# Moving transfers within one issue queue: q tiles two iterations later, the w2 pieces, g2T and pqT at other f chunks, and the first reload of hh in two transfers

## Chip, cores, metric

One core of one Trainium2 chip. The metric is the device time of one execution in microseconds (us); the span of the profile is some 1.7 us shorter. A difference under 2% counts as "same"; the 95% intervals say which differences are clear of noise. One kernel's executions differ by several us from chip to chip and from run to run (the kernel before: 854.9 to 856.5 on one chip). So times are compared only with the kernel before in the same rounds on the same chip, and parts of a microsecond are read from the traces, stretch by stretch.

## The reference

A transformer layer, forward and backward, in bf16, S = 2048 rows, D = 640, 32 heads, F = 1728:

```
h   = x + linear_attention(layernorm(x)) @ wo     # phi(q), phi(k), phi(k)^T v per head
out = h + (silu(n @ w1) * (n @ w3)) @ w2           # n = layernorm(h)
return out, gradients of x, wqkv, wo, w1, w3, w2   # for a given grad_out
```

## The kernel before

The schedule is written by hand. Nearly all DMAs are issued by SP in program order (`dma`, and `dmaT` for a transposing DMA). In the first stage x is normalised, transposed and multiplied by wqkv. From row tile 8 on, the transposes of x (`xn` to `pqT`) are DMAs:

```python
    def p1_norm(t):
        xns[t] = p1.tile([P, D], BF16, name="xn", bufs=4)
        ln1.norm(xns[t][:], x_sb[:, t, :], t)
        if t >= XT_DMA:                                   # 8
            dmaT(out=pqT[:, :, t * P:(t + 1) * P], in_=xns.pop(t)[:])
    # ...
    for t in range(ST):
        # ... k tile, v tile, a kv group every fourth t
        if XT_DMA <= t + 3 < ST:
            p1_norm(t + 3)
        if t + 4 < ST:
            ln1.run(x_sb, t + 4, t + 5)
        if 4 <= t < 12:
            q_tile(t - 4)                                 # ends with a store of pq
        if t in (9, 13):
            load_pqT((t - 9) // 4)                        # transposing reload of 4 stored q tiles
        # ...
        if i == TPC - 1:
            sl = slice(g * TPC, (g + 1) * TPC)
            dma(out=pk_v[:, sl, :], in_=pkc[g][:])
            dma(out=va_v[:, sl, :], in_=va[g % 2][:])
        elif t >= 2 and trickle:
            trickle.pop(0)()                              # one weight load
```

The second stage is the MLP over four chunks c of 512 rows, in 14 f chunks each. Beside it runs the attention output of the next chunk: per row tile `nd` (matmul), `o_t` (DVE), its transpose `oT` (DMA), the out-projection `at` (matmul), `hn` and its transpose.

```python
        for fc in range(FT):
            mlp(c, fc, lambda: run_side(0, fc))
            # ... stores of hh, gate and up are dealt out between these
            run_side(1, fc)
            drain(1)
            if c == 0 and fc in (1, 4, 7):
                a, b = {1: (0, 4), 4: (4, 8), 7: (8, 13)}[fc]
                dma(out=w2[:, a:b, :], in_=B_w2[a * P:b * P, :].rearrange("(c p) n -> p c n", p=P))
                # ...
            if c < 2 and fc == 11:
                load_pqT(c + 2)
            if fc == (9 if c == 0 else 3) and c + 1 < SC:
                load_g2T(c + 1)
            # ...
    def load_hh(b):
        f0, fw = blk[b]
        hb[b] = U2.tile([P, ST, 512], BF16, name="hb", tag="ABCA"[b])
        dmaT(out=hb[b][:, :, 0:fw], in_=hh_d[f0:f0 + fw, :])
    load_hh(0)
```

After that come the gradient of w2 (`gw`, reads hb), the gradient of hn (`ghn`, reads ggb), the attention's gradients (`gwo` and others) and the remaining weight gradients.

Of the kernel before, what the change touches and what calls it, by code (L numbers as in the profile page):

```python
# [9 lines left out]
P = 128  # L10
# [15 lines left out]
W, SC, TPC = 512, 4, 4  # L26
# [37 lines left out]
def kernel(  # L64
# [20 lines left out]
    dma, dmaT = SY.dma_start, SY.dma_start_transpose  # L85
# [18 lines left out]
    hh_d = dram.tile([F, S], BF16, name="hh_d")  # L104
# [68 lines left out]
    def make_mask(m):  # L173
        a, b = M_H[m]
        v = mask[:, m, 0:M_W[m]]
        G.memset(v, 1.0)
        v = v.rearrange("p (h e) -> p h e", e=DA)

        G.affine_select(out=v, in_=v, pattern=[[-DH, b - a], [0, DA]], compare_op=ALU.is_ge, fill=0.0,
                        base=m * P - a * DH, channel_multiplier=1)  # L180
        G.affine_select(out=v, in_=v, pattern=[[DH, b - a], [0, DA]], compare_op=ALU.is_gt, fill=0.0,
                        base=a * DH + DH - m * P, channel_multiplier=-1)
# [9 lines left out]
    def load_g2T(c):  # L192
        g2T[c] = U2.tile([P, DT, W], BF16, name="g2T", tag="g2T", bufs=2)
        dmaT(out=g2T[c][:], in_=goD[c * W:(c + 1) * W, :])

    def load_pqT(c):
        dmaT(out=pqT[:, :, c * W:(c + 1) * W], in_=pq_d[c * W:(c + 1) * W, :])
# [16 lines left out]
# [3 lines that stand above are left out]
        if t >= XT_DMA:  # L217
            dmaT(out=pqT[:, :, t * P:(t + 1) * P], in_=xns.pop(t)[:])

    def p1_tr(t):  # L220
        xn = xns.pop(t)
        tr = ps.tile([P, DT, P], BF16, name="tr", bufs=2)
        for c in range(DT):
            T.transpose(tr[:, c, :], xn[:, c * P:(c + 1) * P], ident[:])

        A.copy(out=pqT[:, :, t * P:(t + 1) * P], in_=tr[:])
# [6 lines left out]
    def p1_mm(t, n0):  # L233
        acc = ps.tile([P, 2, 512], F32, name="big", bufs=3)
        for j in range(2):
            p1_half(acc[:, j, 0:HD], t, n0 + j * HD)
        return acc
# [4 lines left out]
    def phi(acc, dst, relu=False):  # L242
        mq = p1.tile([P, D], BF16, name="mq", bufs=3)
        A.activation(two(mq[:]), acc[:, :, 0:HD], AF.Exp)
        if relu:
            rq = p1.tile([P, D], BF16, name="rq", bufs=3)
            A.activation(two(rq[:]), acc[:, :, 0:HD], AF.Relu)
        V.tensor_scalar(out=mq[:], in0=mq[:], scalar1=1.0, scalar2=1e-6, op0=ALU.min, op1=ALU.add)
        if relu:
            V.tensor_tensor(out=dst, in0=mq[:], in1=rq[:], op=ALU.add)  # L250
            return
        V.scalar_tensor_tensor(out=two(dst), in0=acc[:, :, 0:HD], scalar=0.0, in1=two(mq[:]), op0=ALU.max,
                               op1=ALU.add)

    def q_store(t, pq):
        dma(out=pq_v[:, t, :], in_=pq)

    def q_tile(t):
        pq = p1.tile([P, D], BF16, name="pq", bufs=3)
        phi(p1_mm(t, 0), pq[:], True)  # L260
        q_store(t, pq[:])

    def kv_group(g, last):
        kv = ps.tile([P, 2, 512], F32, name="big", bufs=3)
        for i in range(TPC):
            for m, (a, b) in enumerate(M_H):
                bank, off = KV_SLOT[m]
                T.matmul(kv[:, bank, off:off + M_W[m]], lhsT=pkc[g][:, i, m * P:(m + 1) * P],
                         rhs=va[g % 2][:, i, a * DA:b * DA], start=(i == 0 and off == 0), stop=(i == TPC - 1),
                         skip_group_check=True)  # L270
        for bank, w in ((0, sum(M_W[0:3])), (1, sum(M_W[3:5]))):
            if g == 0:
                V.tensor_copy(out=kvacc[:, bank, 0:w], in_=kv[:, bank, 0:w])
            else:
                V.tensor_tensor(out=kvacc[:, bank, 0:w], in0=kvacc[:, bank, 0:w], in1=kv[:, bank, 0:w],
                                op=ALU.add)
        if last:
            for m, (a, b) in enumerate(M_H):
                bank, off = KV_SLOT[m]
                V.tensor_tensor(out=kvbd[:, m, a * DA:b * DA], in0=kvacc[:, bank, off:off + M_W[m]],  # L280
                                in1=mask[:, m, 0:M_W[m]], op=ALU.mult)
# [22 lines left out]
    for t in range(ST):  # L304
        g, i = divmod(t, TPC)
        if i == 0:
            pkc[g] = p1.tile([P, TPC, D], BF16, name="pkc", bufs=2)
        k = p1_mm(t, D)
        if t + 2 < XT_DMA:
            p1_norm(t + 2)  # L310
        phi(k, pkc[g][:, i, :])
        if t + 1 < XT_DMA:
            p1_tr(t + 1)
        if i == 0 and g > 0:
            kv_group(g - 1, False)
        v = p1_mm(t, 2 * D)
        A.copy(out=va[g % 2][:, i, 0:C].rearrange("p (j h e) -> p j h e", j=2, e=DA)[:, :, :, 0:DH],
               in_=v[:, :, 0:HD].rearrange("p j (h e) -> p j h e", e=DH))
        if XT_DMA <= t + 3 < ST:
            p1_norm(t + 3)  # L320
        if t + 4 < ST:
            ln1.run(x_sb, t + 4, t + 5)
        if 4 <= t < 12:
            q_tile(t - 4)
        if t in (9, 13):
            load_pqT((t - 9) // 4)
        if 2 <= t < 2 + DT:
            make_mask(t - 2)
            G.memset(kvbd[:, t - 2, :], 0.0)
# [5 lines that stand above are left out]
            trickle.pop(0)()  # L335
# [150 lines left out]
    def drain(n):  # L486
        for _ in range(min(n, len(later))):
            later.pop(0)()
# [74 lines left out]
    for c in range(SC):  # L563
        hhT[c] = pa.tile([P, FT, W], BF16, name="hhT", bufs=2)
        o2 = o2_steps(c - 1) if c > 0 else None

        def run_side(pos, fc):
            if c + 1 < SC:
                for f, i in sorted(sides[c][pos].get(fc, ()), key=lambda x: x[1]):
                    f((c + 1) * TPC + i)  # L570
# [4 lines that stand above are left out]
            if o2 and not (c == SC - 1 and fc == 5):  # L575
                next(o2, None)
            run_side(1, fc)
            drain(1)
            if c == 0 and fc in (1, 4, 7):
                a, b = {1: (0, 4), 4: (4, 8), 7: (8, 13)}[fc]  # L580
                dma(out=w2[:, a:b, :], in_=B_w2[a * P:b * P, :].rearrange("(c p) n -> p c n", p=P))
                if fc == 7:
                    dma(out=w2[0:FL, FT - 1, :], in_=B_w2[(FT - 1) * P:F, :])
            if c < 2 and fc == 11:
                load_pqT(c + 2)
            if fc == (9 if c == 0 else 3) and c + 1 < SC:
                load_g2T(c + 1)
            if c == SC - 1 and fc == 0:
                g2 = U1.tile([P, ST, D], BF16, name="g2", tag="Q")
                tail = U2.tile([P, DT, P], BF16, name="w13tail", tag="g2T", bufs=2)  # L590
            if c == SC - 1 and fc in (1, 2, 5, 6):
                i = (1, 2, 5, 6).index(fc)
                dma(out=g2[:, i * TPC:(i + 1) * TPC, :], in_=goS[:, i * TPC:(i + 1) * TPC, :])
            if c == SC - 1 and fc == 8:
                dma(out=tail[:, :, 0:FL], in_=B_w1[:, F - FL:F].rearrange("(c p) f -> p c f", p=P))
                dma(out=tail[:, :, FL:P], in_=B_w3[:, 0:P - FL].rearrange("(c p) f -> p c f", p=P))
            if c == SC - 1 and fc == 9:
                woT = U1.tile([P, DT, D], BF16, name="woT", tag="W6")
                dmaT(out=woT[:], in_=A_wo[:, :])
# [5 lines left out]
    hb, blk = {}, [(0, 512), (512, 512), (1024, 512), (1536, 192)]  # L605

    def load_hh(b):
        f0, fw = blk[b]
        hb[b] = U2.tile([P, ST, 512], BF16, name="hb", tag="ABCA"[b])
        dmaT(out=hb[b][:, :, 0:fw], in_=hh_d[f0:f0 + fw, :])  # L610

    load_hh(0)
    for _ in o2_steps(SC - 1, A.dma_start, "nd"):
        drain(1)
# [56 lines left out]
    for fc in range(FT - 1):  # L671
        b, i = divmod(fc, 4)
# [252 lines left out]
    a, b, c = ST - 1, ST - 2, ST - 3  # L925
# [103 lines left out]
    for t in range(ST):  # L1029
        c, i = divmod(t, TPC)  # L1030
# [124 lines left out]
```

## Time and profile before

| | before |
|---|---|
| time, median | 855.38 us (854.9 to 856.47, 4 runs) |
| span of the profile | 852.4 us |
| TensorE busy | 837.7 us |
| waits of TensorE that the change can reach | xn 1.4, hb 1.1, g2T 0.6, nd 0.3 us |

TensorE does almost nothing but work. What is left are gaps of about 1 us where it waits for one transfer, and the prediction below quotes them. A line of waits reads: engine, what it wanted to do, the line, what it waited for, then the sum, the number and the longest. PE is TensorE, DVE VectorE, ACT ScalarE, and SPq the queue of SyncE, here called SP.

### The profile page before, as it was taken

The page shows a single profiled execution, that of the slowest core. Times are in us where ns is not written, and L with a number is a line of the kernel's source. Part 1 is how long each engine was busy: PE and PEld are TensorE (multiplying, and loading weights), DVE is VectorE, ACT ScalarE, POOL GpSimd, SP SyncE. Part 2 cuts the span into 40 slices and gives each one's busy share as a digit, 9 for nine tenths or more (in the row PEclk, how much of TensorE's full clock was granted, in tenths as well). Part 3 has the DMA queues.
Part 4 walks back from the last instruction along what each step waited for, and adds up shares of the span by engine and source line. Part 5 has one row for each costly group of instructions (what it writes and reads, how often), then busy time and mean ns, then how long its engine had stood idle before and what let it go on. Part 6 is the DMA issues. An engine that isn't in the chain of part 4 may idle for free.

```text
span 852.4 us, 14861 instructions
## 1 busy us (share of the span) xinstructions
PE 837.7 (98%) x5908; PEld 543.3 (64%) x5908; DVE 415.5 (49%) x951; ACT 322.2 (38%) x608; POOL 31.7 (4%) x57
## 2 busy tenths in 40 slices
PE   6999999999999999999999999999999999999998
PEld 4776654555555555677777777777877777655554
DVE  7876698777778566200146666554413343300000
ACT  4656866555555665011111211122522333311111
POOL 2510000000000000000000000000000000000000
PEclk9999999999999999999999999999999999999999
DMA  9999379465574555999679999979666887677671
GB/s 284 270 303 268 104 209 240 140 176 142 128 192 128 156 176 157 242 232 255 181 167 187 204 204 208 172 143 264 145 132 128 191 199 162 159 168 155 154 175 37
DMA packets 344949, 156.35 MB, mean 183 GB/s; under 512 B 247600, under 2 KB 343600, under 8 KB 344880
## 3 DMA queue, kind: packets, MB, share of 16 engines
q1 hardware_dynamic: 316064, 142.45, 69.5%
q10 hardware_dynamic: 28816, 12.97, 7.9%
q8 instruction: 46, 0.75, 0.4%
q14 instruction: 23, 0.19, 0.1%
HBM read 45.20 MB, written 50.02 MB: 112 GB/s over the span
## 4 chain that ended last, share of the span: by engine, by line
PE 81%; DMA 6%; DVE 2%; ACT 1%; ACTq 0%; issue 0%; SPq 0%; DVEq 0%
PE job L986 21%; PE mm L429 18%; PE ghn L734 9%; PE gxn L1076 8%; PE gw L678 7%; PE o L520 6%; PE gwo L841 3%; PE at L386 2%; DMA ggb<-gg_d 2%; PE h L791 2%; DMA hb<-hh_d 2%; DMA ghT<-g_h 1%; PE mm L230 1%; PE dkv L1035 1%; PE dkv L822 1%; DMA pqT<-pq_d 1%
## 5 line engine op out<-in xcount | busy, mean ns | idle before, releaser
L986 PE MATMUL job<-gb,hnN 128*128 128x432 bf16 x640 | 117.0, 346 | 0.0
L734 PEld LDWEIGHTS <-ggb 128*128 128x128 bf16 x864 | 83.0, 98 | 31.9 <-DMA ggb<-gg_d 1.1
L986 PEld LDWEIGHTS <-hnN 128*128 128x128 bf16 x640 | 62.6, 98 | 54.1
L429 PE MATMUL mm<-pqT,w 128*128 128x512 bf16 x405 | 96.1, 379 | 0.0
L429 PEld LDWEIGHTS <-w 128*128 128x128 bf16 x540 | 52.4, 98 | 60.7 <-issue 0.2
L990 ACT CAST obs<-job 128x432 bf16<-128x432 f32 (+1 forms) x70 | 33.3, 475 | 123.8 <-PE job L986 123.8
L429 PE MATMUL mm<-g2T,w2T 128*128 128x512 bf16 x280 | 69.6, 379 | 0.6 <-DMA g2T<-in_grad_out_dram 0.6
L520 PE MATMUL o<-w,hhT 128*128 128x320 bf16 x448 | 67.5, 299 | 0.0
L1076 PE MATMUL gxn<-wqT,gT 128*128 128x320 bf16 x480 | 67.3, 299 | 0.0
L734 PE MATMUL ghn<-w13a,ggb 128*128 128x320 bf16 x448 | 65.6, 299 | 0.0
L734 PE MATMUL ghn<-w13b,ggb 128*128 128x320 bf16 x416 | 63.5, 299 | 0.6 <-DMA ggb<-gg_d 0.4
L230 PE MATMUL big<-wqkv,pqT 128*128 128x320 bf16 x400 | 57.8, 303 | 2.3 <-DMA pqT<-xn 1.4
L230 PEld LDWEIGHTS <-pqT 128*128 128x128 bf16 x480 | 46.5, 99 | 20.9 <-DMA pqT<-xn 2.1
L520 PEld LDWEIGHTS <-hhT 128*128 128x128 bf16 x448 | 43.8, 98 | 23.6
L678 PE MATMUL gw<-g,hb 128*128 128x320 bf16 x416 | 57.7, 299 | 1.1 <-DMA hb<-hh_d 1.1
L1076 PEld LDWEIGHTS <-gT 128*128 128x128 bf16 x480 | 47.0, 98 | 18.2
L986 PEld LDWEIGHTS <-g 128*128 128x128 bf16 x480 | 46.6, 98 | 17.5
L446 ACT CAST ghh<-mm 128x512 bf16<-128x512 f32 x56 | 32.8, 586 | 64.3 <-PE mm L429 63.9
L757 ACT ACTIVATE y<-wb,s,ln_rs 128x640 bf16<-128x640 f32 x32 | 29.4, 920 | 66.5 <-DVE wb L753 66.5
L678 PEld LDWEIGHTS <-hb 128*128 128x128 bf16 x416 | 40.2, 98 | 16.6 <-DMA hb<-hh_d 1.4
L745 ACT ACTIVATE gs<-ghn 128x640 bf16<-128x640 f32 x16 | 11.3, 704 | 88.6 <-PE ghn L734 74.0
L460 ACT ACTIVATE sig<-mm 128x512 bf16<-128x512 f32 x56 | 33.5, 598 | 28.8 <-PE mm L429 27.7
(139 smaller groups left out, 1062.3 us busy)
## 6 DMA issues: line engine op xcount, KB each, us to landing
hh_d<-hhT SPq DMA_DIRECT2D x24, 256.0 KB, 2.5
gg_d<-gate SPq DMA_DIRECT2D x24, 256.0 KB, 2.5
gg_d<-up SPq DMA_DIRECT2D x24, 256.0 KB, 2.5
ggb<-gg_d SPq DMA_DIRECT2D x6, 896.0 KB, 8.0
ggb<-gg_d SPq DMA_DIRECT2D x6, 832.0 KB, 8.2
out_dram<-obs ACTq DMA_DIRECT2D x40, 108.0 KB, 1.9
ggb<-gg_d SPq DMA_DIRECT2D x2, 1728.0 KB, 13.0
va_d<-va SPq DMA_DIRECT2D x4, 768.0 KB, 6.6
```

What stands on the lines that cost most here:

```text
L230: T.matmul(acc, lhsT=pqT[:, c, t * P:(t + 1) * P], rhs=wqkv[:, c, n0:n0 + HD], start=(c == 0), stop=(c == DT - 1))
L429: T.matmul(acc[:], lhsT=w[:, c, fc * P:(fc + 1) * P], rhs=rhs[:, c, :], start=(c == 0), stop=(c == DT - 1))
L446: A.copy(out=ghh[n // 2][:, n % 2, :], in_=acc[:])
L460: A.activation(sig[:, i, :], gp[:], AF.Sigmoid)
L520: T.matmul(o2["ps"][:, 0:HD], lhsT=hhT[c][:, fc, i * P:(i + 1) * P], rhs=w2[:, fc, j * HD:(j + 1) * HD], start=(fc == 0), stop=(fc == FT - 1))
L678: T.matmul(acc[:, j, 0:HD], lhsT=hb[b][:, t, i * P:(i + 1) * P], rhs=g2[:, t, j * HD:(j + 1) * HD], start=(t == 0), stop=(t == ST - 1))
L734: T.matmul(acc[:, j, 0:HD], lhsT=ggb[t // 2][:, k, lo:lo + P], rhs=rhs[:, j * HD:(j + 1) * HD], start=(k == 0), stop=(k == NG - 1))
L757: A.activation(out=y[:], in_=wb[:], func=AF.Identity, bias=s[:, 3:4], scale=st.rs[:, t:t + 1])
L841: T.matmul(acc[m][:, j, 0:HD], lhsT=o_sb[:, t, m * P:(m + 1) * P], rhs=g_h[:, t, j * HD:(j + 1) * HD], start=(t == 0), stop=(t == ST - 1))
L986: T.matmul(acc[:, 0:n], lhsT=lhs[:, t, m * P:(m + 1) * P], rhs=rhs(t), start=(t == 0), stop=(t == ST - 1))
L990: A.copy(out=ob, in_=acc[:, 0:n])
L1076: T.matmul(acc[:, j, 0:HD], lhsT=gT[t][:, k, :], rhs=wqT[:, k, j * HD:(j + 1) * HD], start=(k == 0), stop=(k == 14))
```

## The change

Its intent is to give four transfers more lead. Nothing is computed differently.

```diff
-        if 4 <= t < 12:
-            q_tile(t - 4)
-        if t in (9, 13):
-            load_pqT((t - 9) // 4)
+        if 6 <= t < 14:
+            q_tile(t - 6)
+        if t in (11, 15):
+            load_pqT((t - 11) // 4)
@@
-                a, b = {1: (0, 4), 4: (4, 8), 7: (8, 13)}[fc]
+                a, b = {1: (0, 5), 4: (5, 9), 7: (9, 13)}[fc]
@@
-            if c < 2 and fc == 11:
+            if c < 2 and fc == 10 - 2 * c:
                 load_pqT(c + 2)
-            if fc == (9 if c == 0 else 3) and c + 1 < SC:
+            if fc == (5 if c == 0 else 3) and c + 1 < SC:
                 load_g2T(c + 1)
@@ load_hh
-        dmaT(out=hb[b][:, :, 0:fw], in_=hh_d[f0:f0 + fw, :])
+        for a, n in ((0, 2 * P), (2 * P, 2 * P)) if b == 0 else ((0, fw),):
+            dmaT(out=hb[b][:, :, a:a + n], in_=hh_d[f0 + a:f0 + a + n, :])
```

## The prediction

> **What bounds the kernel now.** I read the page's header first, then the waits of TensorE, then the same engine's timeline around each wait, and last the timeline of SP, the queue that issues nearly all DMAs in program order.
>
> ```profile
> span 852.4 us, 14861 instructions
> PE 837.7 (98%) x5908; PEld 543.3 (64%) x5908; DVE 415.5 (49%) x951; ACT 322.2 (38%) x608; POOL 31.7 (4%) x57
> PE 81%; DMA 6%; DVE 2%; ACT 1%; ACTq 0%; issue 0%; SPq 0%; DVEq 0%
> ```
>
> TensorE is busy for 837.7 of 852.4 us at a granted clock of 1.00. The change adds and removes no matmul, so all that it can win is idle time of TensorE: 852.4 - 837.7 = 14.7 us, 1.7% of the span. Even the whole of it would not be 2%. The waits say how much of it the change can reach:
>
> ```profile
> PE tr L224 <- DVE xn L145: 5.6, 1, 5.6
> PE big L230 <- DMA pqT<-xn: 1.4, 2, 1.1
> PE gw L678 <- DMA hb<-hh_d: 1.1, 1, 1.1
> PE big L230 <- ACT pqT L226: 0.8, 1, 0.8
> PE mm L429 <- DMA g2T<-in_grad_out_dram: 0.6, 1, 0.6
> PE at L386 <- DVE o_t L362: 0.5, 1, 0.5
> PE ghn L734 <- DMA ggb<-gg_d: 0.4, 1, 0.4
> PE nd L349 <- DMA pqT<-pq_d: 0.3, 1, 0.3
> ```
>
> The 5.6 and the 0.8 us are the start of the kernel (first x and its normalisation), and 121.00 - 116.84 = 4.2 us lie after the last matmul (the stretch from 732 to 853 us); the change touches neither. Four of these waits are in its reach: xn (1.4), hb (1.1), g2T (0.6), nd (0.3), 3.4 us in all, 0.4% of the time. So the question is only which of these go, and what new wait a moved transfer makes.
>
> [...] the transpose of hb is 8.52 us on SP but lands 13.0 us after its start. [...] SP issues in program order, and one long transpose there (w2T, 15.17 us) holds back all issues behind it.
>
> **Part 1, q tiles two iterations later.** A q tile is ten matmuls at a pitch of 1.36/10 us, so 1.36 us of TensorE. They leave iterations 4 and 5 and appear in 12 and 13. From iteration 4 to 13 TensorE runs up to 2 x 1.36 = 2.7 us ahead of before, and from iteration 14 on it stands where it stood, less the waits saved. The timeline before:
>
> ```profile
> 59.45 1.52 PE L230 MATMUL big<-wqkv,pqT 128*128 128x320 bf16 x10
> 61.33 5.61 PE L230 MATMUL big<-wqkv,pqT 128*128 128x320 bf16 x40 [0.36 <-DMA pqT<-xn]
> 68.02 2.89 PE L230 MATMUL big<-wqkv,pqT 128*128 128x320 bf16 x20 [1.07 <-DMA pqT<-xn]
> ```
>
> Those waits are for the DMA transposes of x tiles 13 and 15. On SP tile 13's was issued at 55.51 and landed 5.8 us later, at 61.3; tile 15's at 61.60, landing 6.4 us later, at 68.0. Tile 13's was held back by the reload of pqT chunk 0 (issued at 51.16, 3.63 us on SP). This reload now comes two iterations later, so tile 13 is issued near 49.5, lands near 55, and TensorE asks for it at 59.5 (counting 1.36 us a half-tile group and 1.33 a kv group from 23.64): that wait goes. Tile 8 becomes tighter: TensorE asks for it at 36.4 instead of 39.1; before, it was issued at 32.61 behind the g2T transpose, which itself stood behind the first q store. Without that store it is issued near 30.3 and lands near 35, so no wait, with 1.5 us to spare.
>
> But the reload of chunk 0 now stands ahead of tile 15. It follows the store of q tile 5, whose matmuls end at 54.1; from the end of such matmuls to the reload's issue it took 2.6 us before (48.6 to 51.16), so the reload is issued near 56.6 and done near 60.3. Then come the stores of pk and va (about 0.6 us each), and tile 15 is issued near 61.5, as before, landing near 68.0. TensorE would ask at 66.3, now 0.65 us sooner. So I expect one wait of about 1.7 us for tile 15 in place of 0.36 + 1.07 and the two small start-up losses beside them (0.15 each): **about 0.0 us** for the stage, between -1.7 (the wait vanishes) and +0.8.
>
> **Part 2, transfers among the f chunks of the first c.** g2T for chunk 1 moves from f chunk 9 to 5. Before, it was issued at 137.26, landed 5.5 us later, and TensorE waited:
>
> ```profile
> 129.55 1.52 PE L386 MATMUL at<-wo,oT 128*128 128x320 bf16 x10 [0.46 <-DVE o_t L362]
> 142.78 1.25 PE L429 MATMUL mm<-g2T,w2T 128*128 128x512 bf16 x5 [0.64 <-DMA g2T<-in_grad_out_dram]
> 150.84 0.53 PE L349 MATMUL nd<-kvbd,pqT 128*128 128x147 bf16 x6 [0.33 <-DMA pqT<-pq_d]
> ```
>
> Issued some 15 us sooner it is there in time: -0.64 us. The reload of pqT chunk 2 goes from f chunk 11 to 10, some 5 us sooner, against a wait of 0.33: -0.33 us. For c = 1 the reload (now f chunk 8) had no wait to lose: 0. The w2 pieces (5, 4, 4 instead of 4, 4, 5) have no wait of their own: 0.
>
> The new place of g2T costs something. Its issue follows the store of hh at 121.21 on SP, just ahead of this:
>
> ```profile
> 121.21 0.37 SPq L479 DMA_DIRECT2D hh_d<-hhT  x1
> 122.17 0.37 SPq L411 DMA_DIRECT2D hn_d<-hn  x1
> 123.64 0.34 SPq L364 DMA_DIRECT2D o_d<-o_t  x1
> 124.27 0.39 SPq L479 DMA_DIRECT2D gg_d<-gate  x1
> 124.75 1.24 SPq L419 DMA_TRANSPOSE pqT<-hn  x1
> 126.05 1.27 SPq L370 DMA_TRANSPOSE oT<-o_t  x1
> ```
>
> g2T takes SP from 121.7 to 125.2. The gaps between these lines take up part of it; packed back to back (0.45 + 0.4 + 0.45 + 1.3 us) the oT transpose starts near 127.9 to 128.2 instead of 126.05. It landed 2.6 us after issue, so near 130.7 instead of 128.65. The out-projection of row tile 6 started at 129.55 (held by the DVE read of a PSUM bank), so it now starts about 1.2 us later: **+1.2 us**. Part 2 in sum: -0.64 - 0.33 + 1.2 = +0.2.
>
> **Part 3, first reload of hh in two transfers.** Its issue at 341.94 needs the last reader of w1; 13.0 us later the whole block lands, and the gradient of w2 starts at 355.04 after 1.1 us of idle. The first two f chunks need only the first half. Half the columns take about 8.52/2 = 4.3 us on SP and land another 13.0 - 8.5 = 4.5 us later, so near 350.7, while TensorE is done with its earlier work at 353.9. The second half lands near 355, and is first read two f chunks of 4.5 us later. The wait goes: **-1.1 us**. hb 1 was queued from 352.19 and is first needed at 373.1, so there is room behind.
>
> **Sum.** 0.0 + 0.2 - 1.1 = -0.9 us, mostly kept, as the later stages show only one other wait of TensorE for a DMA (0.4 us for ggb), and that transfer waits for buffers which TensorE frees, so it moves along. 855.24 - 0.9 = 854.3 us.
>
> **Rivals.** (a) All four waits vanish and nothing takes their place: -3.4, so 851.8 us. For it: each moved transfer gets more lead. Against it: SP is one queue, and in the first stage the DMA share is above 1 (1.14 from 50 to 60 us, 1.17 from 60 to 70), so what is moved back must delay something. (b) The new places hurt: the oT delay is 2 us and passes on to row tile 7 (whose oT landed 6.2 us after 130.87, at 137.07, against a use at 137.38), and tile 15 lands 1 us later. Then +0.8 + 0.9 (above the 1.2) + 0.3 offset the gain, and the time is about 854.3 + 2.0 = 856.3. For it: the margins of 0.3 and 0.9 us there. (c) The split is hidden or fails to help because the first gw matmul waits for both halves: +1.1 on the estimate, 855.4. Against it: chunks of pqT written by separate DMAs are awaited separately in this trace.
>
> **Range and chances.** From (a) to (b), with the three timed runs spread over 854.9 to 856.47, I give 852.2 to 856.4. 2% is 17.1 us, five times all waits within reach, and above all idle of TensorE; a loss of that size would need a DMA wait of a kind the trace nowhere shows. Faster 0.005, same 0.99, slower 0.005.
>
> **What would show it.** In the waits of TensorE after: hb gone, g2T and nd gone, "at" grown to 1.5 us or more and ended by oT's DMA, xn down to one wait of 1.2 to 2 us near 66 us. The oT transpose issued about 7 us after the hh store instead of 4.8. If "at" stays at 0.5, part 2 is wrong and the time is nearer 853.1; if no xn wait is left, part 1 is wrong and it is nearer 852.6. A gw wait still there would mean that the split does not free the first half.

## The result, and the profile after

855.23 us (853.45 to 856.71, 4 runs) against 855.38 us: ratio 0.9996, 95% interval 0.9973 to 1.0018. Ratios here are the mean time of one kernel's runs over that of the other's of the same rounds, so not quite the ratio of the medians. A second set of six runs (below) gave 0.9977 (0.9959 to 0.9994).

The waits of TensorE in the changed kernel:

```profile
PE tr L224 <- DVE xn L145: 5.7, 1, 5.7
PE at L386 <- DMA oT<-o_t: 2.5, 1, 2.5
PE big L230 <- ACT pqT L226: 0.8, 1, 0.8
PE h L823 <- DVE gnd L794: 0.7, 1, 0.7
PE big L230 <- DMA pqT<-xn: 0.6, 1, 0.6
```

hb, g2T and nd are gone, and xn is down from 1.4 to 0.6. The wait at the out-projection of row tile 6 grew from 0.5 to 2.5 us, and what ends it is no longer DVE but the DMA of oT. TensorE's timeline shows the three places (columns: start, length, what, and in brackets the idle time before it):

```profile
67.40 2.89 PE L230 MATMUL big<-wqkv,pqT 128*128 128x320 bf16 x20 [0.59 <-DMA pqT<-xn]
...
130.99 1.53 PE L386 MATMUL at<-wo,oT 128*128 128x320 bf16 x10 [2.51 <-DMA oT<-o_t]
...
353.94 4.51 PE L679 MATMUL gw<-g,hb 128*128 128x320 bf16 x32
```

And SP's timeline in the changed kernel shows why:

```profile
120.60 0.37 SPq L479 DMA_DIRECT2D hh_d<-hhT  x1
121.03 3.31 SPq L194 DMA_TRANSPOSE g2T<-in_grad_out_dram  x1
124.43 0.53 SPq L411 DMA_DIRECT2D hn_d<-hn  x1
...
127.32 1.27 SPq L370 DMA_TRANSPOSE oT<-o_t  x1
```

g2T keeps SP for 3.31 us, everything behind it is packed tight, and oT is issued 6.7 us after the hh store instead of 4.8 us. That is 1.9 of the 2.9 us by which oT lands later, counted from the hh store (10.35 instead of 7.48 us); the other 1.0 us is a longer time from issue to landing (3.6 instead of 2.6 us).

To see where time goes in all runs alike, I took from each timeline of TensorE the start of four groups of matmuls: the first late q tile, the first output matmul of chunk 0 (`o`), the first `gw`, `ghn` and `gwo`. Between them lie these stretches (us). From gw to ghn it is 60.3 us, and from gwo to the end 290.7 to 290.8 us, in every run; both are left out. "dip" says whether the granted clock fell in the 10 us from 130 us.

| run | q at / reload at | g2T at f chunk | split | start to late q | late q to o | dip | o to gw | ghn to gwo |
|---|---|---|---|---|---|---|---|---|
| before | 4 / 9 | 9 | no | 72.07 | 80.21 | no | 202.76 | 146.39 |
| changed | 6 / 11 | 5 | yes | 71.46 | 80.96 | no | 201.52 | 146.67 |
| e1_g2t_back | 6 / 11 | 9 | yes | 71.27 | 81.61 | no | 201.52 | 146.29 |
| e4_g2t_alone | 4 / 9 | 5 | no | 73.16 | 84.22 | 0.83 | 202.31 | 146.63 |
| e2_q_alone | 6 / 11 | 9 | no | 72.94 | 80.70 | no | 202.51 | 146.44 |
| e3_split_alone | 4 / 9 | 9 | yes | 73.10 | 79.89 | no | 201.52 | 148.11 |
| e8_g2t_fc8 | 6 / 11 | 8 | yes | 71.45 | 80.74 | no | 201.52 | 150.08 |
| e5_g2t_fc4 | 6 / 11 | 4 | yes | 72.13 | 82.17 | no | 201.52 | 146.25 |
| e6_reload_t12 | 6 / 12 | 5 | yes | 71.32 | 83.40 | 0.83 | 201.52 | 147.80 |
| e9_double | 6 / 11 | 5, doubled | yes | 73.09 | 85.53 | 0.83 | 201.52 | 146.59 |
| a1_after_again | 6 / 11 | 5 | yes | 71.20 | 83.00 | 0.83 | 201.52 | 147.32 |
| a2_after_nosplit | 6 / 11 | 5 | no | 71.89 | 83.32 | 0.83 | 202.71 | 146.48 |
| b1_order_split | 6 / 12 | 8 | yes | 70.63 | 80.11 | no | 201.52 | 146.62 |
| b2_order_nosplit | 6 / 12 | 8 | no | 70.95 | 81.27 | no | 203.02 | 146.32 |

### The profile page after: what moved, and what is told of

Read it like the earlier page. It is cut to its first block, busy times and chain, and to the rows that moved or that the text cites. A ratio compares the mean times of both kernels' runs of the same rounds, so it can differ in the third digit from the quotient of the medians.

```text
span 851.7 us, 14834 instructions
## 1 busy us (share of the span) xinstructions
PE 835.9 (98%) x5880; PEld 543.4 (64%) x5908; DVE 415.2 (49%) x951; ACT 322.1 (38%) x608; POOL 31.7 (4%) x57
## 4 chain that ended last, share of the span: by engine, by line
PE 86%; DMA 2%; DVE 1%; issue 0%; ACTq 0%; ACT 0%; SPq 0%
PE job L987 21%; PE mm L429 20%; PE ghn L735 11%; PE gxn L1077 8%; PE o L520 7%; PE gw L679 7%; PE at L386 3%; PE gwo L842 3%; PE h L792 2%; DMA ghT<-g_h 1%; PE mm L230 1%; PE dkv L1036 1%; DMA kT<-pk_d 1%; PE dkv L823 1%; PE nd L349 1%; PE h L823 1%
```

## The experiments

My theory: each part of the change wins its wait, and what it gives back comes from the order of issues on SP alone. The rivals: the transferred bytes themselves slow the neighbours wherever they stand; another part (the w2 pieces) makes the new wait; the split's gain is given back in later stages.

**e1_g2t_back** (ratio 1.0014, 0.9963 to 1.0065; one of its four runs took 862.5 us)

```diff
-            if fc == (5 if c == 0 else 3) and c + 1 < SC:   # changed kernel
+            if fc == (9 if c == 0 else 3) and c + 1 < SC:
```

> The changed kernel with g2T for chunk 1 put back to f chunk 9, everything else kept. Theory A (the g2T transpose on SP holds back the oT transpose of row tile 6): the wait of TensorE at the out-projection of tile 6 falls from 2.5 us to about 0.5 us, oT is issued about 4.8 us after the hh store (6.7 us in the changed kernel), and the g2T wait of about 0.6 us at chunk 1 comes back. Net some -1.4 us by the trace, about 850.3 us of span at full clock. Theory B (the w2 pieces of 5, 4, 4 or the later reload in the first stage made that wait): it stays near 2.5 us and the time rises by 0.6 us.

The wait at the out-projection is back at 0.46 us and the one for g2T at 0.63 us, so the w2 pieces and the later reload don't make the 2.5 us. But the net gain that I expected did not come, for a wait that I had not foreseen. TensorE's timeline of this run:

```profile
128.87 1.52 PE L386 MATMUL at<-wo,oT 128*128 128x320 bf16 x10 [0.46 <-DVE o_t L362]
...
142.09 1.25 PE L429 MATMUL mm<-g2T,w2T 128*128 128x512 bf16 x5 [0.63 <-DMA g2T<-in_grad_out_dram]
...
149.24 1.24 PE L429 MATMUL mm<-g2T,w2T 128*128 128x512 bf16 x5 [1.58 <-ACT up L468]
```

With g2T at f chunk 9 and the reload of pqT at 10, two transposes follow each other on SP (3.45 us from 136.59 and 3.81 us from 140.71). The store of up behind them comes at 144.62, ACT waits 2.5 us for its buffer, and TensorE 1.58 us for ACT. In this trace the parts of the change belong together: the earlier reload needs g2T out of the way.

**e4_g2t_alone** (1.0055, 1.0031 to 1.0078: slower than before, clear of noise)

```diff
-            if fc == (9 if c == 0 else 3) and c + 1 < SC:   # kernel before
+            if fc == (5 if c == 0 else 3) and c + 1 < SC:
```

> The kernel before with only g2T for chunk 1 moved from f chunk 9 to 5. Theory A: the g2T wait (0.6 us) goes and the wait at the out-projection of row tile 6 grows from 0.5 to about 2.4 us: net about +1.3 us, span near 853.7 us at full clock; the nd wait of 0.3 us goes too if freeing SP around 137 us lets the reload of pqT start sooner, and stays if not. Theory B: the out-projection wait stays at 0.5 us and the time falls by 0.6 us.

The wait grew to 2.88 us, a little more than forecast, but the kernel lost 4.3 us between the medians, not 1.3; the stretch from late q to o alone is 4.0 us longer (84.22 against 80.21). The g2T wait is gone; the nd wait became 1.03 us. And there is something that no wait shows: in the stretches of 10 us, the granted clock is 0.83 from 130 us on, and nowhere else in the span. The matmuls after the long wait ran slower (1.88 us for ten that take 1.52, 2.34 us for five that take 1.24).

**e2_q_alone** (1.0016, 0.9994 to 1.0038)

```diff
-        if 4 <= t < 12:                 # kernel before, other parts unchanged
-            q_tile(t - 4)
-        if t in (9, 13):
-            load_pqT((t - 9) // 4)
+        if 6 <= t < 14:
+            q_tile(t - 6)
+        if t in (11, 15):
+            load_pqT((t - 11) // 4)
```

> The kernel before with only the q tiles and their reloads two iterations later. Theory A (TensorE bound, the reload of pqT chunk 0 ahead of the tiles is what cost): two xn waits of 1.4 us in sum become one of about 0.6 us at tile 15, as in the changed kernel, and the first matmul of the late q tiles starts 0.6 us sooner than before; net -0.6 us. Theory B (the gain came by another part, or by chance from run to run): the xn waits keep a sum of 1.4 us or more.

One xn wait is left, as forecast, but it is 1.93 us, so by this run alone theory B would stand. Eight runs have the q tiles at 6 and the reload at 11; their xn waits are 0.6, 0.4, 1.9, 0.4, 0, 0.9, 0 and 0.2 us. The three with the old order have 1.4, 2.1 and 2.1 us. The late q tiles start at 71.93 us in the mean of the eight and at 72.78 us in the mean of the three: a gain of about 0.85 us, with a scatter of the same size. A single trace was too few here.

**e3_split_alone** (1.0012, 0.9990 to 1.0033)

```diff
-        dmaT(out=hb[b][:, :, 0:fw], in_=hh_d[f0:f0 + fw, :])   # kernel before
+        for a, n in ((0, 2 * P), (2 * P, 2 * P)) if b == 0 else ((0, fw),):
+            dmaT(out=hb[b][:, :, a:a + n], in_=hh_d[f0 + a:f0 + a + n, :])
```

> The kernel before with only the first reload of hh in two transfers. Theory A: the gw wait of 1.1 us goes, the first gw matmul follows the last output matmul at once (near 354.0 instead of 355.0), and 1.1 us of it is still there at the first matmul of the next stage and most at the end: span near 851.3 us. Theory B (later transfers take it back): SP's 10.7 us for the two transfers against 8.5 us for one delay w13 and ggb, the first matmul of the next stage waits, and the span is 852.4 us as before.

The gw wait is gone, and the stretch from o to gw is 201.52 us: the same to the hundredth in all nine runs with the split, and 202.31 to 203.02 in the five without. But here the ghn stage took 148.11 instead of 146.39 us, with waits of 1.3 us for ghT and 0.7 for gnd, and the gain was gone at the end. Whether that follows from the split is asked again below.

**e8_g2t_fc8** (0.9961, 0.9931 to 0.9991)

```diff
-            if fc == (5 if c == 0 else 3) and c + 1 < SC:   # changed kernel
+            if fc == (8 if c == 0 else 3) and c + 1 < SC:
```

> The changed kernel with g2T for chunk 1 at the end of f chunk 8, behind the oT transposes of row tiles 6 and 7 in SP's order, instead of 5. Theory A (only the order of SP's issues makes the wait at the out-projection of tile 6): that wait falls from 2.5 to about 0.5 us, no wait for g2T (it lands near 137 us and is read near 142), none for the reload of pqT chunk 2; from there on some 2 us sooner than the changed kernel, span near 849.8 us with the granted clock at 1.00 in every 10 us. Theory B (the g2T transfer itself slows the oT transfer, wherever it stands): the wait moves to tile 7, of 1 us or more, and the span is 851 us or more.

The wait at tile 6 is 0.47 us, none is at tile 7, none for g2T or the reload, and no dip. So the same bytes, sent 11 us later but still in good time, cost nothing: what counts is its place in the order. (By this run alone, the order of issues on SP and the order of the bytes in the DMA queues are not told apart; e9 below does more.) The span of the profiled run was nevertheless 854.9 us. TensorE's timeline of that run shows where most of it went, far from the change:

```profile
148.55 1.24 PE L429 MATMUL mm<-g2T,w2T 128*128 128x512 bf16 x5 [0.70 <-ACT up L468]
...
491.68 1.26 PE L735 MATMUL ghn<-w13b,ggb 128*128 128x320 bf16 x8 [3.16 <-DMA ggb<-gg_d]
```

The reload of ggb has waits of 0 to 3.2 us from run to run, in a stage with a DMA share near or above 1 (1.28 from 475 us in this run). This is one cause of the scatter; the six runs of this kernel go from 851.16 to 858.47 us.

**e5_g2t_fc4** (1.0003, 0.9975 to 1.0031)

```diff
-            if fc == (5 if c == 0 else 3) and c + 1 < SC:   # changed kernel
+            if fc == (4 if c == 0 else 3) and c + 1 < SC:
```

> The changed kernel with g2T for chunk 1 at f chunk 4, where SP stood idle for 3.7 us (117.5 to 121.2 us in the kernel before). Theory A (order on SP alone): the out-projection wait of tile 6 is about 0.5 us, since SP is free again before the hh store. The price is the store of up, which stands behind g2T and comes some 3.5 us later; if ACT then waits for its buffer and TensorE for ACT, a wait of TensorE for ACT of up to 1 us appears near 122 to 126 us. Span 849.8 to 851 us. Theory B (transfer itself): oT of tile 6 lands late all the same and the wait stays above 1.5 us.

The out-projection wait is 0.49 us, as theory A has it, but the price was larger than I allowed. SP's and TensorE's timelines:

```profile
117.06 5.20 SPq L194 DMA_TRANSPOSE g2T<-in_grad_out_dram  x1
122.37 0.53 SPq L479 DMA_DIRECT2D gg_d<-up  x1
```

```profile
127.58 1.24 PE L429 MATMUL mm<-pqT,w 128*128 128x512 bf16 x5 [2.98 <-ACT up L468]
```

Here g2T took 5.20 us on SP instead of 3.3, right behind a w2 piece. The store of up came at 122.37, ACT waited 4.3 us for its buffer, and TensorE 2.98 us for ACT. An idle gap of SP isn't free when a store that somebody waits for stands behind it.

**e6_reload_t12** (0.9985, 0.9961 to 1.0009)

```diff
-        if t in (11, 15):               # changed kernel
-            load_pqT((t - 11) // 4)
+        if t in (12, 15):
+            load_pqT((t - 12) // 3)
```

> The changed kernel with the first reload of pqT one iteration later (12 instead of 11), so behind the transpose of x tile 15 in SP's order. Theory A (the reload ahead of tile 15 makes the xn wait): no xn wait is left (0.6 us in the changed kernel, 1.9 us in the run with the q part alone), and the late q tiles start 0.6 us sooner, near 70.9 us. Theory B (the DMA engines are the limit there, not the order): a wait of 0.5 us or more stays. Everything behind as in the changed kernel, the wait of 2.5 us at the out-projection too.

No xn wait is left here, nor in the two later runs with this order. SP's timeline shows the new order, tile 15 ahead of the reload:

```profile
59.93 1.96 SPq L218 DMA_TRANSPOSE pqT<-xn  x1
62.59 0.35 SPq L256 DMA_DIRECT2D pq_d<-pq  x1
63.03 3.06 SPq L197 DMA_TRANSPOSE pqT<-pq_d  x1
```

The late q tiles started at 71.32 us, not at 70.9; in the three runs with this order they start at 70.97 us in the mean, 1.0 us before those with the reload at 11. The clock dip is there again, behind a wait of 2.81 us.

**e9_double** (1.0026, 0.9995 to 1.0058)

```diff
-            if c < 2 and fc == 10 - 2 * c:   # changed kernel
+            if (c == 0 and fc == 5) or (c == 1 and fc == 8):
                 load_pqT(c + 2)
```

> The changed kernel with the reload of pqT chunk 2 put right behind g2T at f chunk 5: the suspected cost (transpose issues of SP ahead of oT of tile 6) doubled. Theory A: oT is issued about 3 us later still, the wait at the out-projection grows from 2.5 to about 5.5 us, and the granted clock falls below 1.00 in the 10 us behind it, as in the run with g2T alone (0.83 there after 2.9 us of idle), costing another 1.5 to 2 us: span 856 to 857.5 us, mean clock 0.998. Theory B (SP's order is not what counts, or the wait of 2.5 us is set by something else): the wait stays near 2.5 us and the span near 852.

In fact the reload stands just ahead of g2T, not behind, which is the same for oT. SP is taken for 3.75 + 3.25 us, oT is issued 10.4 us after the hh store (6.7 in the changed kernel, 4.8 before), the wait is 5.31 us, and the clock falls to 0.83 from 130 us. Dose and response agree with theory A. Here oT landed 2.7 us after its issue, as in the kernel before, though twice the bytes had gone ahead of it: bytes ahead do not by themselves slow it.

**a1_after_again, a2_after_nosplit, b1_order_split, b2_order_nosplit** (same chip, same rounds). a1 is the changed kernel; b1 has g2T at f chunk 8 (as e8) and the reload at 12 (as e6); a2 and b2 have the hh reload in one transfer:

```diff
-        for a, n in ((0, 2 * P), (2 * P, 2 * P)) if b == 0 else ((0, fw),):   # a1, b1
-            dmaT(out=hb[b][:, :, a:a + n], in_=hh_d[f0 + a:f0 + a + n, :])
+        dmaT(out=hb[b][:, :, 0:fw], in_=hh_d[f0:f0 + fw, :])                  # a2, b2
```

> The changed kernel once more, beside the three others of this call. Theory A (its time hangs on whether the wait at the out-projection of tile 6 trips the granted clock): the wait is 2.3 to 2.9 us again; runs with a mean granted clock of 0.998 or less are 1.5 to 2 us longer than runs at 1.000, and against the kernel before the mean is within 1 us. Theory B (the wait was a chance of one run): it is near 0.5 us here.

> The changed kernel with the first reload of hh in one transfer again. Theory A (the split's 1.1 us is kept): the first gw matmul waits 0.6 to 1.1 us for hb, the stretch from the first ghn to the first gwo matmul is as long as in the changed kernel, and the run is about 1 us longer than the changed kernel of this call. Theory B (the gain is given back in the ghn stage, where the DMA share is above 1): the stretch from ghn to gwo is near 146.5 us here, as in the three runs without the split (146.39, 146.44, 146.63), against 146.3 to 150.1 us in the seven with it, and the times of the two are alike or this one is faster.

> The changed kernel with both places set by SP's order: g2T for chunk 1 at f chunk 8 and the first reload of pqT at iteration 12. Theory A: no xn wait, 0.5 us at the out-projection of tile 6, no clock dip near 130 us; up to 0.7 us of waiting for ACT near 148 us is left; time 2.5 to 3.5 us (0.3 to 0.4%) below the kernel before of the same rounds and below the changed kernel by 2 us or more. Theory B: jitter of the ghn stage (waits for ggb from 0 to 3.2 us from run to run) covers it, and the interval includes 1.

> The same with the first reload of hh in one transfer. Theory A (the split's gain is kept): 1 us longer than the run with the split. Theory B (given back): the same or shorter, with a stretch from ghn to gwo near 146.5 us.

| | median of 6 runs, us | ratio to before | 95% interval |
|---|---|---|---|
| before | 857.09 (11 runs) | | |
| a1 changed kernel | 855.90 | 0.9977 | 0.9959 to 0.9994 |
| a2 without the split | 857.13 | 0.9998 | 0.9980 to 1.0017 |
| b1 both places by SP's order | 851.90 | 0.9934 | 0.9916 to 0.9952 |
| b2 the same, without the split | 854.05 | 0.9957 | 0.9938 to 0.9975 |

The wait at tile 6 in a1 is 2.73 us, and the dip is there. The stretches of two microseconds behind it (columns: stretch, its length, busy time and number of TensorE, weight loads, DVE, ACT and GpSimd, granted clock, DMA share, GB/s), first in the changed kernel's first profile, then in a1:

```profile
130.00:132.00 2.00, 1.01 (x8) 0.74 (x9) 0.46 (x2) 0.31 (x1) 0.00 (x0) 1.00 0.95 258
132.00:134.00 2.00, 2.00 (x12) 1.03 (x11) 1.78 (x5) 0.63 (x2) 0.00 (x0) 1.00 0.99 299
134.00:136.00 2.00, 1.95 (x10) 0.88 (x9) 1.89 (x5) 1.51 (x4) 0.92 (x1) 1.00 1.94 302
```

```profile
130.00:132.00 2.00, 0.91 (x6) 0.65 (x7) 0.20 (x1) 0.23 (x1) 0.00 (x0) 0.92 0.94 266
132.00:134.00 2.00, 2.00 (x8) 0.93 (x7) 1.05 (x3) 0.35 (x1) 0.00 (x0) 0.50 0.86 212
134.00:136.00 2.00, 2.00 (x8) 0.85 (x7) 1.90 (x6) 0.58 (x1) 0.76 (x1) 0.73 1.06 374
```

TensorE is "busy" alike in both, but in a1 the clock is 0.92, 0.50 and 0.73. The lost part is 2 x (0.08 + 0.50 + 0.27) = 1.7 us; the stretch from late q to o is 83.00 - 80.96 = 2.04 us longer, of which 0.2 us is the longer wait. Read in stretches of 0.2 us, the clock is 0.50 for 3.4 us in each of the five traces with a dip (a1, a2, e4, e6, e9); the 0.83 over 10 us that all five show is the same loss, 10 x 0.17 = 1.7 us. The first profile of the changed kernel happened to be a run without the dip. Of the ten runs of the changed kernel, eight have a mean granted clock of 0.998 or less and take 856.0 us in the mean; the two at 1.000 took 853.45 and 853.95 us. A mean clock of 0.998 is a loss of 0.002 x 854 = 1.7 us, one such dip. (Of these eight only a1's was profiled; that the others dip at the same place is inferred.)

In b1 the placement alone is worth 0.9934 against 0.9977, 0.43% or 3.7 us. Its waits:

```profile
PE tr L224 <- DVE xn L145: 5.7, 1, 5.7
PE mm L429 <- ACT up L468: 1.0, 1, 1.0
PE ghn L735 <- DMA ggb<-gg_d: 0.9, 1, 0.9
PE big L230 <- ACT pqT L226: 0.8, 1, 0.8
PE at L386 <- DVE o_t L362: 0.5, 1, 0.5
PE h L823 <- DMA gndT<-gnd: 0.2, 1, 0.2
```

The split is kept: both pairs, a and b, differ by about 0.2% in its favour (0.9998 - 0.9977 and 0.9957 - 0.9934), some 1.8 us, and the traces without it show the hb wait of 1.0 and 1.3 us. The rival isn't wholly wrong: the stretch from ghn to gwo is 146.32 to 146.63 us in the five runs without the split and 146.25 to 150.08 us in the nine with it, 0.85 us more in the mean. In the timed pairs this does not outweigh the gain. b1 is faster than both kernels, clear of noise though under 2%. Against the kernel before, a1 and b1 did better than expected (2.0 and 5.7 us by the ratios; the expectations were within 1 us and 2.5 to 3.5 us). The spans of the profiled runs show only 2.4 us between b1 and the kernel before (850.0 and 852.4); the kernel before was slower in these rounds (857.09 us), for which there is no trace.

## Why the prediction was right

The time lay in the range, and "within 2%" was safe for the reason given: the change adds no work to TensorE and could reach only 3.4 us of waits. The measured gain, 0.15 us between the medians at first and 1.2 us in the second set, lies on both sides of the forecast 0.9 (by the ratios: 0.3 and 2.0 us). The first interval includes no change at all, so this agreement alone proves little. Within that, some steps held and some did not.

- **Part 3 held.** Forecast -1.1 us; from o to gw it is 1.14 us less (202.66 in the mean without, 201.52 with). The forecast for the first half was a landing after 4.3 + 4.5 = 8.8 us; it took 9.2, and that half landed at 351.3 us. I took the SP time to be the same in sum; the two transfers need 10.68 us there instead of 8.52.
- **g2T and nd held.** Both waits (0.64 and 0.33 us) are gone in the changed kernel. By e1 they belong together, which I had not said.
- **The new wait at the out-projection held in kind, not in size.** I forecast 1.2 us more from an issue at 127.9 to 128.2 and a landing 2.6 us later. The issue came at 127.32, but the landing took 3.6 us, and TensorE was 0.6 us earlier. The wait grew by 2.05 us (2.51 - 0.46). The mis-sized term is the landing: 3.3 to 3.7 us in the five runs with g2T alone at f chunk 5, 3.2 in e5, and 2.6 to 2.7 in the other eight, e9 among them. Why is open.
- **The step that was missing: what a wait does to the clock.** I counted a wait of some 1.7 us as 1.7 us. In eight of ten runs, by their mean clock, it costs about 1.7 us more, since the granted clock falls. The five traces with a dip agree in size: 0.50 for 3.4 us, 1.7 us lost. What sets it off they don't settle: the waits in front of it took 2.73 to 2.88 us, and 5.31 in e9, all longer than the 1.7 us that I expected, while 2.51 us in the changed kernel's first profile brought no fall. The trace of the kernel before, at 1.00 in every 10 us, gave no warning, and I had reckoned only with what the DMAs cost.
- **Part 1 was mis-sized.** I forecast 0.0 us, between -1.7 and +0.8, and measured about -0.85 in the mean of eight runs against three. Two of its terms held: tile 15's transpose was issued at 61.47 us (forecast 61.5), and the wait for tile 13 went. But it landed in 5.9 us, not 6.4, and TensorE asked at 66.8, later than 66.3, so that 0.59 us was left instead of 1.7. Tile 8 was not as free as I said: g2T took 6.00 us on SP, not 3.6, so tile 8 was issued at 32.86 instead of 30.3, and 60 matmuls there took 8.59 us against 8.31 to 8.39 in the other runs.
- **Rival (b) was nearer than I allowed** for the second stage (the wait of 2 us more), and rival (a) for the first. They happened to cancel, which is part of why the sum was right. Rival (c) fell: the first gw matmul started at 353.94 us, when its own half had landed and the second, at 355.3, had not.
- **A small slip.** The 4.2 us after the last matmul come from a stretch that ends 0.6 us behind the span; the last matmul ended at 848.84 of 852.4 us, so it is 3.6 us. Nothing rests on it.

What stays open: why oT's landing took 1 us longer, what the w2 pieces are worth (they were not run alone; by e1 they don't make the new wait), why the ghn stage with its ggb and ghT transfers scatters more with the split, and why the kernel before itself goes from 853.2 to 860.6 us on one chip at a mean clock of 0.998 to 1.000. The jitter of ggb is one cause, shown in e8; I have no trace of a long run of the kernel before. With the part 1 and part 3 gains, the second-stage loss and the mean ghn loss added up from the traces (-0.85 - 1.14 + 2.4 + 0.85 = +1.3 us; 2.4 is the mean of the four runs of the changed second stage, 82.67, less 80.27 of the three with the old one), the changed kernel should be a little slower than before, while it was timed 0.3 and 2 us faster; the few traces of the old order do not carry a balance to one microsecond.

## What to carry to other kernels

Here, where one queue issues nearly all DMAs in order, moving a long transpose forward was paid for by what stood behind it: oT was issued 1.9 us later behind g2T at f chunk 5, and ACT waited 4.3 us for the store of up behind it at 4 (e5). In such a queue look for the first issue that somebody waits for, a transpose or a store that frees a buffer, and put the long one just behind that (g2T at f chunk 8 left 0.47 us of wait at tile 6, against 0.46 before). When TensorE is the bound, don't count a wait only by its length: read the granted clock in the few microseconds after it (0.50 for 3.4 us in five traces here). And where transfers scatter by a microsecond (the xn waits of the eight runs with q at 6 and the reload at 11 go from 0 to 1.9 us), take several traces of each order and compare the same stretch between two matmuls, not one pair of spans.

## What the traces say of the clock, the split and SP's issues

- The clock: idle gaps of TensorE of 2.73, 2.81, 2.85 and 2.88 us were each followed by the dip, and so was e9's of 5.31 us, while 2.51 us was not, and neither were 2.98 us (e5) and 3.16 us (e8). Four of the six gaps between 2.7 and 3.2 us set it off; their length alone does not tell which. Depth and length of the fall are alike in all five traces that show it (0.50 for 3.4 us).
- The split: what it costs is time of the issuing queue. The two halves took 10.68 us on SP (10.36 in e3) against 8.52 us for the one transfer.
- SP's issues: the same transpose does not take the same time there. That of g2T took 3.31 us on SP with little ahead of it and 5.20 us right behind a w2 piece. The one for chunk 0 took 6.00 us behind the w2T transpose: issued 2.1 us earlier than in the kernel before (26.76 against 28.90), it left SP no sooner (32.76 against 32.52) and landed no sooner (36.3 against 36.1). That transfers ahead are the cause is inferred, and not every one counts: right behind the pqT reload in e9 it took 3.25 us. In the changed kernel an xn transpose took 1.21 to 2.90 us.
